# A spectral layer beside a two-layer FFN on one core: the transform reordered with a fold, gelu in one activation, and the instruction order made by a list scheduler

## Chip, cores, metric

One NeuronCore of one Trainium2 chip. The metric is the device time of one execution in microseconds; medians of several runs are quoted.

## The reference, cut to what matters

```python
x = A_x                                   # 1 x 2048 x 640, bf16
xn = layernorm(x)                         # over the 640 features
# A: a filter in the frequency plane
X = rfft2(xn)                             # 2048 x 321, complex
y = irfft2(X * (w_r + 1j * w_i)).astype(bf16)
# B: two dense layers, 640 -> 1536 -> 640
h = gelu(xn @ w1 + b1)                    # tanh form
out = x + y + (h @ w2 + b2)
```

The Fourier transforms are matrix products with constant tables. The sequence of 2048 is taken as 128 x 16, so its transform has two stages.

## The kernel before

Five engines run hand-ordered lists of instructions. Tiles of 128 sequence positions are normalised, transposed, taken through the feature transform (complex from there on) and the first sequence stage; then come transposes of the filter and of the data, the second stage with the filter, two inverse stages, and an output product in which 18 matmuls (12 of the FFN, 6 of the inverse feature transform) are summed per half. Two quarters of the first FFN product are woven into the middle as items of fixed places. The parts that the argument touches:

```python
# x: tiles 0..3, then the tables and W1 in the same queue; tile 4 only when tile 0 is normalised
for c in range(4):
    load_x_tile(c, c)
... etab; gtab; bdtab; b1t; W1sb ...
def act_normalize(c):
    ... activation(Identity, bias=nmr, scale=rstd) ...
    if c + 4 < 16:
        W("sp", act_xn, n)
        load_x_tile(c + 4, xs)

# one FFN item: a product, and the gelu of the items before it, in stages
def ffn_item(t):
    ... five matmuls of 512 columns ...
    activation(hb, PB[bnk], ACT.Identity, bias=b1col)          # item t
    activation(sg, ub, ACT.Sigmoid, scale=GSCALE)              # item t-2
    tensor_tensor(h2, hb, hb, mult)                            # item t-1
    tensor_scalar_add(ub, h2, A22)
    tensor_tensor(ub, ub, hb, mult)
    tensor_tensor(gT, hb, sg, mult)                            # item t-3

# the order: chain items in fixed sequence, one ffn_item after every third or so
chain = [T x11] + [B2C x11] + [Da x21] + [Db x24]
```

Of the kernel before, what the change touches and what calls it, by code (L numbers as in the profile page):

```python
# [6 lines left out]
dt = mybir.dt  # L7
ACT = mybir.ActivationFunctionType
ALU = mybir.AluOpType

S = 2048
D = 640
F = 1536
KP = 328
NG = 41
NDC = 5
NFC = 12
NT1 = 48
GSCALE = 2.0 * float(np.sqrt(2.0 / np.pi)) * 0.044715
A22 = 1.0 / 0.044715  # L20


def _bf16_bits(a):
    a = np.ascontiguousarray(a, dtype=np.float32)
    u = a.view(np.uint32).astype(np.uint64)
    r = ((u + 0x7FFF + ((u >> 16) & 1)) >> 16).astype(np.uint16)
    return r


def _make_tables():  # L30
    T = {}
    d = np.arange(D)[:, None].astype(np.float64)
    k = np.arange(KP)[None, :].astype(np.float64)
    valid = (np.arange(KP) < 321)[None, :]
    Ec = np.cos(2 * np.pi * ((d * k) % D) / D) * valid
    Es = -np.sin(2 * np.pi * ((d * k) % D) / D) * valid
    Etab = np.concatenate([Ec, Es], axis=1)
    T["Etab"] = Etab.reshape(NDC, 128, 2 * KP).transpose(1, 0, 2)
    s1 = np.arange(128)[:, None, None].astype(np.float64)
    s2 = np.arange(16)[None, :, None].astype(np.float64)  # L40
    m1 = np.arange(128)[None, None, :].astype(np.float64)
    ang = 2 * np.pi * ((m1 * (16 * s1 + s2)) % 2048) / 2048.0
    Gc, Gs = np.cos(ang), np.sin(ang)
    T["Gtab"] = np.concatenate([Gc, Gs, -Gs], axis=2)
    m1b = np.arange(128)[:, None, None].astype(np.float64)
    s2b = np.arange(16)[None, :, None].astype(np.float64)
    s1b = np.arange(128)[None, None, :].astype(np.float64)
    angH = 2 * np.pi * ((m1b * (16 * s1b + s2b)) % 2048) / 2048.0
    Hc, Hs = np.cos(angH), np.sin(angH)
    T["Htab"] = np.concatenate([-Hs, Hc, Hs], axis=2)  # L50
    qin = np.arange(128)
    s2_in = qin // 8
    kk_in = qin % 8
    qout = np.arange(128)
    m2_out = qout // 8
    kk_out = qout % 8
    delta = (kk_in[:, None] == kk_out[None, :]).astype(np.float64)
    ang16 = 2 * np.pi * ((s2_in[:, None] * m2_out[None, :]) % 16) / 16.0
    T["BDtab"] = np.concatenate([delta * np.cos(ang16), delta * np.sin(ang16), -delta * np.sin(ang16)], axis=1)
    q = np.arange(128)  # L60
    m2q = q // 8
    kkq = q % 8
    col = np.arange(128)
    s2c = col // 8
    kkc = col % 8
    delta2 = (kkq[:, None] == kkc[None, :]).astype(np.float64)
    ang16b = 2 * np.pi * ((m2q[:, None] * s2c[None, :]) % 16) / 16.0
    T["BD2tab"] = np.concatenate([-delta2 * np.sin(ang16b), delta2 * np.cos(ang16b), delta2 * np.sin(ang16b)], axis=1)
    kk_ = np.arange(384)[:, None].astype(np.float64)
    dd = np.arange(D)[None, :].astype(np.float64)  # L70
    kidx = np.arange(384)
    ck = np.where((kidx == 0) | (kidx == 320), 1.0, 2.0)[:, None]
    validk = (kidx < 321)[:, None]
    angE = 2 * np.pi * ((kk_ * dd) % D) / D
    GEr = ck * np.cos(angE) / (S * D) * validk
    GEi = -ck * np.sin(angE) / (S * D) * validk
    GE = np.stack([GEr, GEi], axis=1)
    T["GEtab"] = GE.reshape(3, 128, 2, D).transpose(1, 0, 2, 3)
    T["ident"] = np.eye(128)
    return T  # L80


class Chan:

    def __init__(self, nc, name, inc=1):
        self.sem = nc.alloc_semaphore(name)
        self.n = 0
        self.inc = inc

    def next(self):  # L90
        self.n += self.inc
        return self.n


def bass_parallel_sum__spectral_gfnet__dense_activation_gelu__prompt_kernel(
# [11 lines left out]
    T = _make_tables()  # L107
    c_etab = nc.inline_tensor(_bf16_bits(T["Etab"]), name="c_etab")
    c_gtab = nc.inline_tensor(_bf16_bits(T["Gtab"]), name="c_gtab")
    c_htab = nc.inline_tensor(_bf16_bits(T["Htab"]), name="c_htab")  # L110
    c_bd = nc.inline_tensor(_bf16_bits(np.concatenate([T["BDtab"], T["BD2tab"]], axis=1)), name="c_bd")
    c_ge = nc.inline_tensor(_bf16_bits(T["GEtab"]), name="c_ge")
    c_ident = nc.inline_tensor(_bf16_bits(T["ident"]), name="c_ident")

    x2 = A_x[0]
    xv = x2.rearrange("(p c) d -> c p d", c=16)
    ov = out[0].rearrange("(p c) d -> c p d", c=16)
    wrv = A_w_r.rearrange("(m2 p) k -> p m2 k", p=128)
    wiv = A_w_i.rearrange("(m2 p) k -> p m2 k", p=128)
# [5 lines left out]
    ops = {"pe": [], "act": [], "dve": [], "pool": [], "sp": []}  # L125

    def E_(eng, f):
        ops[eng].append(f)
    pe = lambda f: E_("pe", f)
    act = lambda f: E_("act", f)  # L130
    dve = lambda f: E_("dve", f)
    pool = lambda f: E_("pool", f)
    sp = lambda f: E_("sp", f)

    def W(eng, ch, n):
        if n <= 0:
            return
        ops[eng].append(lambda e, s=ch.sem, n=n: e.wait_ge(s, n))

    with ExitStack() as es:  # L140
        sb = lambda name, shape, dtype=dt.bfloat16: es.enter_context(nc.sbuf_tensor(name, shape, dtype))
        ident = sb("ident", [128, 128])
        bdtab = sb("bdtab", [128, 768])
        b1t = sb("b1t", [NFC, 128])
        b1col = sb("b1col", [128, NFC], dt.float32)
        gT = sb("gT", [128, NFC, S])
        stats = sb("stats", [128, 16, 12], dt.float32)
        mv = sb("mv", [128, 16, 2], dt.float32)
        stdv = sb("stdv", [128, 16], dt.float32)
        rstd = sb("rstd", [128, 16], dt.float32)  # L150
        nmr = sb("nmr", [128, 16], dt.float32)
        epsv = sb("epsv", [128, 1], dt.float32)
        warm = sb("warm", [128, 1], dt.float32)
        R4N = 17920
        R4 = sb("R4", [128, R4N])
        xnT = bass.AP(tensor=R4, offset=0, ap=[[R4N, 128], [1, 10240]]).rearrange("p (c s) -> p c s", c=NDC)
        W1sb = bass.AP(tensor=R4, offset=10240, ap=[[R4N, 128], [1, 7680]]).rearrange("p (c f) -> p c f", c=NDC)

        R1N = 32912
        R1 = sb("R1", [128, R1N])  # L160

        def r1(off, n):
            return bass.AP(tensor=R1, offset=off, ap=[[R1N, 128], [1, n]])
        o = 0
        W2g = r1(o, 10496).rearrange("p (r g m k) -> p r g m k", r=2, g=NG, m=16); o += 10496
        xring = r1(o, 4 * D).rearrange("p (j d) -> p j d", j=4); o += 4 * D
        xnring = r1(o, 4 * D).rearrange("p (j d) -> p j d", j=4); o += 4 * D
        etab = r1(o, NDC * 656).rearrange("p (c x) -> p c x", c=NDC); o += NDC * 656
        gtab = r1(o, 16 * 384).rearrange("p (s x) -> p s x", s=16); o += 16 * 384
        xdring = r1(o, 4 * 656).rearrange("p (j r k) -> p j r k", j=4, r=2); o += 4 * 656  # L170
        wnring = r1(o, 2 * 2 * 4 * KP).rearrange("p (j r m k) -> p j r m k", j=2, r=2, m=4); o += 2 * 2 * 4 * KP
        assert o <= R1N, o
        Zsb = r1(0, 10496).rearrange("p (r g m) -> p r g m", r=2, g=NG)
        T2T = r1(10496, 10496).rearrange("p (r g m) -> p r g m", r=2, g=NG)
        Vsb = r1(20992, 10496).rearrange("p (s r k) -> p s r k", s=16, r=2)
        getab = r1(0, 3 * 2 * D).rearrange("p (c r d) -> p c r d", c=3, r=2)
        UT = [r1(3840 + kc * 4096, 4096).rearrange("p (r s a) -> p r s a", r=2, s=16) for kc in range(3)]
        htabA = r1(16128, 8 * 384).rearrange("p (s x) -> p s x", s=8)
        ysb = r1(20992, 2 * 1024).rearrange("p (j x) -> p j x", j=2)
        stg_off = 20992  # L180
        xrring = r1(stg_off, 3 * D).rearrange("p (j d) -> p j d", j=3)
        ostg = r1(stg_off + 3 * D, 3 * D).rearrange("p (j d) -> p j d", j=3)
        R2N = 10496
        R2 = sb("R2", [128, R2N])
        T2sb = bass.AP(tensor=R2, offset=0, ap=[[R2N, 128], [1, 10496]]).rearrange("p (r g s k) -> p r g s k", r=2, g=NG, s=16)
        W2sb = bass.AP(tensor=R2, offset=0, ap=[[R2N, 128], [1, NFC * D]]).rearrange("p (c e) -> p c e", c=NFC)
        ctmp = bass.AP(tensor=R2, offset=NFC * D, ap=[[R2N, 128], [1, 4 * 512]]).rearrange("p (j x) -> p j x", j=4)
        assert NFC * D + 4 * 512 <= R2N
# [10 lines left out]
        def pbb(i):  # L199
            return PB[i][:].bitcast(dt.bfloat16)  # L200

# [740 lines left out]
```

## Time and profile before

| | before |
|---|---|
| time, median of 4 runs | 262.42 us (261.89 to 262.99) |
| profiled span | 259.0 us |
| TensorE busy / matmuls | 218.0 us / 1507 |
| VectorE, ScalarE busy | 157.8, 121.4 us |
| first x tile to fifth x tile usable | 3.5 to 22.5 us |

TensorE's busy time overstates how full the engine is (a transpose of 128 columns has a record of 219 ns, and the next one starts after 56). One more view is needed below, the groups by shape, where the gelu stands as six rows (columns: busy us, mean ns of one, idle of the engine before them):

```profile
L562 ACT ACTIVATE hb<-pb,b1col 128x512 bf16<-128x512 f32 x48 | 34.7, 723 | 46.9 <-PE pb L272 46.6
L572 ACT ACTIVATE sg<-ub 128x512 bf16<-128x512 bf16 x48 | 31.9, 665 | 5.2 <-DVE ub L590 5.1
L584 DVE TENSOR_TENSOR h<-hb 128x512 bf16<-128x512 bf16 x48 | 20.0, 416 | 6.2 <-ACT hb L562 6.2
L587 DVE TENSOR_SCALAR ub<-h 128x512 bf16<-128x512 bf16 x48 | 15.2, 316 | 1.6
L590 DVE TENSOR_TENSOR ub<-ub,hb 128x512 bf16<-128x512 bf16 x48 | 20.4, 425 | 1.6
L599 DVE TENSOR_TENSOR gT<-hb,sg 128x512 bf16<-128x512 bf16 x48 | 20.0, 418 | 0.1
```

These six rows are 76 us of VectorE and 67 us of ScalarE. They cost time only where one of those two engines sets the pace.

### The profile page before, as it was taken

Reading aid. Unit: us, or ns where it says so; the run is one execution under the profiler, and the core shown is the slowest. Engines: PE = TensorE matmul, PEld = TensorE weight load, DVE = VectorE, ACT = ScalarE, POOL = GpSimd, SP = SyncE. Lnnn points to the kernel's source line nnn. Section 1 sums busy time; section 2 is a strip of 40 time slices with the busy share of each in tenths; the row PEclk is TensorE's granted clock in tenths of the full one; section 3 lists DMA queues with packets and bytes.
Section 4 is the critical chain, followed back from the end, with each engine's and each line's share of the span. In section 5 each row is a group of like instructions: output and inputs, shape, how many; then the busy total and the mean of one; then the engine's idle time right before and its main releaser. Section 6 shows DMA issues by size and latency. Waiting matters only on the chain.

```text
span 259.0 us, 4212 instructions
## 1 busy us (share of the span) xinstructions
PE 218.0 (84%) x1507; PEld 129.2 (50%) x1507; DVE 157.8 (61%) x433; ACT 121.4 (47%) x258; POOL 31.0 (12%) x48
## 2 busy tenths in 40 slices
PE   0703999999959585499299999999999999999995
PEld 0401667768734133266166755545555455655652
DVE  3304688745987999974669996567555774121121
ACT  2500788974148365299848892355323551000000
POOL 8368900000000000000820000000000000000000
PEclk9999999999999977979769999999999999999999
DMA  6999322100009003120400020011101111113101
GB/s 183 385 360 311 107 78 71 35 0 3 3 0 304 0 1 121 16 109 0 152 3 0 1 78 24 26 54 51 51 15 40 51 53 51 53 51 101 53 25 51
DMA packets 10941, 19.89 MB, mean 77 GB/s; under 512 B 1193, under 2 KB 9002, under 8 KB 10794
## 3 DMA queue, kind: packets, MB, share of 16 engines
q1 hardware_dynamic: 10154, 17.00, 20.0%
q0 software_dynamic: 768, 2.63, 3.2%
q8 instruction: 12, 0.20, 0.3%
q14 instruction: 7, 0.06, 0.1%
HBM read 17.01 MB, written 2.62 MB: 76 GB/s over the span
## 4 chain that ended last, share of the span: by engine, by line
PE 57%; DVE 19%; ACT 10%; DMA 7%; issue 5%; DVEq 0%; SPq 0%; ACTq 0%
PE pb L272 57%; DMA R<-in_A_x_dram 7%; ACT R L717 3%; DVE R L529 2%; DVE R L635 2%; ACT R L401 2%; ACT hb L562 2%; DVE R L680 2%; DVE R L689 1%; DVE R L684 1%; DVE R L681 1%; DVE R L682 1%; ACT sg L572 1%; DVE R L428 1%; DVE R L687 1%
## 5 line engine op out<-in xcount | busy, mean ns | idle before, releaser
L272 PE MATMUL pb<-R 128*128 128x512 bf16 (+6 forms) x752 | 138.4, 336 | 23.4 <-DVE R L428 12.5
L272 PEld LDWEIGHTS pb<-R 128*128 128x128 bf16 (+2 forms) x752 | 71.2, 102 | 74.0 <-DVE R L428 13.9
L272 PE MATMUL pb<-R,gT 128*128 128x512 bf16 (+1 forms) x384 | 57.4, 299 | 0.0
L562 ACT ACTIVATE hb<-pb,b1col 128x512 bf16<-128x512 f32 x48 | 34.7, 723 | 46.9 <-PE pb L272 46.6
L854 DVE TENSOR_TENSOR R<-pb,R 128x512 bf16<-128x512 f32 x16 | 11.1, 691 | 52.4 <-issue 42.6
L272 PEld LDWEIGHTS pb<-R,gT 128*128 128x128 bf16 x384 | 30.5, 98 | 24.7
L572 ACT ACTIVATE sg<-ub 128x512 bf16<-128x512 bf16 x48 | 31.9, 665 | 5.2 <-DVE ub L590 5.1
L584 DVE TENSOR_TENSOR h<-hb 128x512 bf16<-128x512 bf16 x48 | 20.0, 416 | 6.2 <-ACT hb L562 6.2
L590 DVE TENSOR_TENSOR ub<-ub,hb 128x512 bf16<-128x512 bf16 x48 | 20.4, 425 | 1.6
L599 DVE TENSOR_TENSOR gT<-hb,sg 128x512 bf16<-128x512 bf16 x48 | 20.0, 418 | 0.1
L358 DVE BATCH_NORM_STATS2 stats<-R 128x6 f32<-128x320 bf16 x16 | 7.7, 484 | 17.1 <-DMA R<-in_A_x_dram 17.1
L272 PE MATMUL pb<-R,bdtab 128*128 128x512 bf16 (+1 forms) x44 | 11.0, 385 | 7.0 <-ACT R L667 3.9
L717 ACT ACTIVATE R<-pb 128x256 bf16<-128x256 f32 x41 | 14.0, 593 | 4.7 <-DVE R L684 4.7
L587 DVE TENSOR_SCALAR ub<-h 128x512 bf16<-128x512 bf16 x48 | 15.2, 316 | 1.6
L401 ACT ACTIVATE R<-R,nmr,rstd 128x640 bf16<-128x640 bf16 x16 | 14.6, 919 | 0.9 <-DVE nmr L389 0.9
L789 POOL MEMSET R<- 32x4096 bf16 x1 | 3.5, 3504 | 91.5 <-PE pb L272 91.5
L420 PE MATMUL pb<-ident,R 128*128 128x128 bf16 x80 | 8.0, 238 | 7.4 <-ACT R L401 7.3
L325 POOL COPY R<-R 128x328 bf16<-128x328 bf16 x32 | 13.1, 466 | 7.1 <-DMA R<-in_A_w_i_dram 7.1
L477 ACT ACTIVATE R<-pb 128x328 bf16<-128x328 f32 x32 | 12.5, 441 | 1.5 <-PE pb L272 0.6
L272 PE MATMUL pb<-bdtab,R 128*128 128x256 bf16 x82 | 12.1, 302 | 0.0
L665 ACT ACTIVATE R<-pb 128x512 bf16<-128x512 f32 (+1 forms) x11 | 6.2, 568 | 12.0 <-DVE R L684 9.8
L447 DVE CAST R<-pb 128x328 bf16<-128x328 f32 x16 | 7.9, 495 | 6.2 <-PE pb L272 5.6
(41 smaller groups left out, 152.5 us busy)
## 6 DMA issues: line engine op xcount, KB each, us to landing
R<-in_A_x_dram SPq DMA_DIRECT2D x32, 160.0 KB, 2.3
R<-in_B_w_dram SPq DMA_DIRECT2D x2, 1920.0 KB, 12.3
out_dram<-R SPq DMA_DIRECT2D x16, 160.0 KB, 1.8
R<-c_gtab SPq DMA_DIRECT2D x1, 1536.0 KB, 9.9
R<-c_htab SPq DMA_DIRECT2D x2, 768.0 KB, 4.2
R<-in_A_w_r_dram POOLq DMA_DIRECT2D x4, 321.0 KB, 7.2
R<-in_A_w_i_dram POOLq DMA_DIRECT2D x4, 321.0 KB, 7.5
R<-c_ge SPq DMA_DIRECT2D x1, 960.0 KB, 4.7
```

Of the source, the lines that this page charges most:

```text
L272: ins = e.matmul(o_, lhsT=lw, rhs=rh, start=st, stop=stp)
L325: ins = e.tensor_copy(W2g[:, ri, :, m2, :], wnring[:, j, ri, ml, :].rearrange("p (g k) -> p g k", k=8))
L401: act(lambda e, c=c, slot=slot, xs=xs: e.activation(xnring[:, slot, :], xring[:, xs, :], ACT.Identity, bias=nmr[:, c:c + 1], scale=rstd[:, ...
L477: ins = e.activation(T2sb[:, ri, :, c, :], PB[bnk][:, 0:KP].rearrange("p (g k) -> p g k", k=8), ACT.Copy)
L562: act(lambda e, bnk=bnk, hs=hs, fc=fc: e.activation(hb[:, hs, :], PB[bnk][:, 0:512], ACT.Identity, bias=b1col[:, fc:fc + 1], scale=1.0).th ...
L572: act(lambda e, us=g4["us"], ss=ss: e.activation(sg[:, ss, :], ub[:, us, :], ACT.Sigmoid, scale=GSCALE).then_inc(act_e4.sem, 1))
L584: dve(lambda e, hs=hs3, h2s=h2s: e.tensor_tensor(out=h2[:, h2s, :], in0=hb[:, hs, :], in1=hb[:, hs, :], op=ALU.mult).then_inc(dve_self.sem ...
L587: dve(lambda e, h2s=h2s, us=us: e.tensor_scalar_add(ub[:, us, :], h2[:, h2s, :], A22).then_inc(dve_self.sem, 1))
L590: dve(lambda e, hs=hs3, us=us: e.tensor_tensor(out=ub[:, us, :], in0=ub[:, us, :], in1=hb[:, hs, :], op=ALU.mult).then_inc(dve_e3.sem, 1))
L599: dve(lambda e, hs=g5["hs"], ss=g5["ss"], fc=g5["fc"], q=g5["q"]: e.tensor_tensor(out=gT[:, fc, 512 * q:512 * (q + 1)], in0=hb[:, hs, :], ...
L717: ins = e.activation(dst, src, ACT.Copy)
L854: dve(lambda e, ba=ba, osl=osl, xs=xs: e.tensor_tensor(out=ostg[:, osl, 0:512], in0=PB[ba][:, 0:512], in1=xrring[:, xs, 0:512], op=ALU.add))
```

## The change

The intent: fewer matmul columns (real data through the first sequence stage; the features folded about their middle, so that sums meet cosines and differences meet sines), one activation per gelu, and an order that a list scheduler computes at build time from estimated durations, instead of one written by hand. Every operation has a priority; at each step the engine that can start first takes its ready operation of highest priority, and slots of PSUM and SBUF are given out in the same pass. The order is then fixed, and each engine is given its list in that order. The diff cut to its core:

```diff
-    T["Etab"] ... T["Gtab"] ... T["BDtab"] ...      # complex, feature transform first
+    T["G"], T["H"], T["E"], T["GE"], T["M"], T["N"] # real sequence stage, folded features
+class Sched: ...                                    # priorities, ready lists, buffer pools, semaphores
+        load_x(0); load ident
+        for j in range(3):
+            load W1 slice j
+            if j == 0: load b1t; load_x(1)
+        load gtab; load_x(2); load_x(3); load etab; load mtab
+        ... 24 loads of the filter, 16 partitions each, in the layout of its use ...
+        load ntab; getab; htab; b2
+        B_b1ps, B_b1c = Buf("b1ps", psum), Buf("b1col")
+        K.op([("pe", 0.1)], 50, ... matmul(b1ps, lhsT=b1t, rhs=ident[0:12, 0:12]))
+        K.op([("dve", 0.2)], 50, ... tensor_copy(b1col, b1ps))
+        # per tile: statistics (priority 100 - g), rstd = (var + eps) ** -0.5 on GpSimd,
+        # normalise, transpose, fold, first sequence stage (priorities 100 - c/2)
+            for k, op in enumerate((ALU.add, ALU.subtract)):
+                tensor_tensor(xf[k], xn[0:320], xn[639:319:-1], op)
+            5 matmuls of 128 columns against gtab[c]
+        # FFN: lowest TensorE priority, fills what is left
+                pr = 10 - q4 - fc / 20
+                5 matmuls of 512 columns
+                activation(gT, hps, ACT.Gelu_apprx_tanh, bias=b1col)       # needs b1col
+        # per column group q of 16: 6 x 320 (features), 4 x 322 (second stage), filter, 10 x 128 (inverse)
+        # per output tile c of 16: 6 x 320 (inverse features), 24 x 320 (FFN) + 4 x 320 (inverse sequence)
-            pipeline of Identity, square, add, multiply, Sigmoid, multiply
-            chain = T, B2C, Da, Db with ffn items at fixed places
```

## The prediction

> **What bounds the kernel now.** I read the page's busy digits first, then stretches of the span, then the chain that ended last, then the groups by shape.
>
> The page:
>
> ```profile
> span 259.0 us, 4212 instructions
> PE 218.0 (84%) x1507; PEld 129.2 (50%) x1507; DVE 157.8 (61%) x433; ACT 121.4 (47%) x258; POOL 31.0 (12%) x48
> PE   0703999999959585499299999999999999999995
> PEclk9999999999999977979769999999999999999999
> ```
>
> The second half is solid TensorE. In the first half there is a hole in slices 0 to 4, and a ragged stretch in slices 11 to 19 where the granted clock falls too. The stretches of the span, split where those change (columns: length, then busy us and count for PE, PEld, DVE, ACT, POOL, then clock, DMA share, GB/s):
>
> ```profile
> 0.00:24.00 24.00, 5.04 (x26) 3.00 (x27) 6.37 (x21) 5.98 (x9) 16.31 (x29) 1.00 0.92 321
> 24.00:60.00 36.00, 35.02 (x272) 24.57 (x271) 25.10 (x75) 27.79 (x60) 7.58 (x18) 1.00 0.21 62
> 60.00:128.60 68.60, 50.73 (x375) 30.35 (x373) 55.93 (x144) 41.66 (x97) 4.69 (x2) 0.91 0.20 67
> 128.60:256.00 127.40, 127.17 (x837) 71.28 (x837) 69.58 (x193) 46.01 (x92) 2.38 (x1) 0.98 0.13 41
> ```
>
> The chain that ended last says what fills each (start, length, what):
>
> ```profile
> 7.29 15.19 DMA R<-in_A_x_dram
> ...
> 61.97 6.26 DVE R L529 x11
> ...
> 128.62 123.25 PE pb L272 x806
> ...
> 255.88 0.69 DVE R L854
> ```
>
> So: (1) until 24 us TensorE waits for x. The fifth tile's load is issued only after tile 0 is normalised, behind the tables and W1 in one queue. (2) 60 to 128.6 us belongs to VectorE and ScalarE: copies of transposes, then six tensor_tensor per group of the filter, with four VectorE and two ScalarE instructions per gelu item in the same strict order. (3) From 128.6 us TensorE alone sets the end, to within 3 us.
>
> A busy TensorE record includes latency, so I price TensorE by spacing. The transposes stand back to back here:
>
> ```profile
> 61.33 4.74 PE L522 MATMUL pb<-ident,R 128*128 128x128 bf16 x82
> ```
>
> (4.74 - 0.22 for the last one's latency) / 81 = 56 ns. Taking starts of consecutive records for the other widths, the median spacing is 216 ns at 512 columns, 139 at 328, 109 at 256[...]. At 320 columns that makes 136, at 322 137.
>
> TensorE work before, in us: x transposes 80 x 56 = 4.5; feature transform 160 x 139 = 22.2; first sequence stage 64 x 139 = 8.9; transposes of filter and data 164 x 56 = 9.2; second stage 8.9; inverse stages 82 x 109 + 96 x 109 = 19.4; first FFN product 240 x 216 = 51.8; output 16 x 18 x (216 + 56) = 78.3. Sum 203. The other 56 of the 259 us are waits, cold clock and the last 3 us.
>
> [...]mean granted clock 0.91 in 60 to 128.6 us and 1.00 in the solid stretch 140 to 256. [...]the trace has 570 ns between biased 512-column PSUM reads and 478 to 495 for plain ones. [...]the trace shows the forward case only (335 ns for 512) and nothing reversed.
>
> **The change part by part.**
>
> *TensorE.* The sequence transform runs first on real data, straight from the normalised tile as weights, so five 128-column matmuls per tile (80 x 56 = 4.5) replace two complex stages. The fold about the middle turns the feature transform into cosine and sine halves: 16 x 6 x 320 columns = 96 x 136 = 13.1. Second sequence stage 64 x 137 = 8.8, its inverse 160 x 56 = 9.0, inverse features 96 x 136 = 13.1, output 16 x 28 x 136 = 60.9, FFN 51.8, x transposes 4.5. Sum 165.6, that is 37 us less. The transposes of filter and data (9.2) are gone, W is loaded in the layout it is used in, and the six spectral matmul pairs per output tile fall to four matmuls.
>
> *ScalarE and VectorE.* Each gelu becomes one biased activation, 48 x 0.57 = 27 us, instead of 48 x (0.57 + 0.52) of ScalarE and 48 x (0.45 + 0.33 + 0.34 + 0.34) = 70 us of VectorE. VectorE keeps bn_stats 32 x 0.39 = 12.6, small ones about 4, normalise 16 x 0.25 = 4, folds 32 x 0.235 = 7.5, filter products 16 x 0.74 = 11.8[...], sums 8 x 1.2 = 9.6, final adds 16 x 0.74 = 11.8: 61 us. Shared: 80 copies of 640 columns from PSUM at 0.585 (ScalarE[...]) or 0.73 (VectorE), and 16 at 0.40: some 58 us. Altogether about 146 us on two engines, 73 each, under half of what TensorE has. They leave the path, except at the head.
>
> *The head.* x now comes in four loads of 640 KB, the first at the front of the queue. The first four 160 KB tiles landed in 3.5 us at first and 640 KB at some 385 GB/s (the page's fastest slice) is 1.7 us, so x arrives about 5.0. Then four tiles of statistics (4 x 0.91), rstd by a power on GpSimd ([...]no record of its cost), normalise 4 x 0.25, three folds, a transpose and a copy: first FFN product near 12 us. The table of the sequence stage lands only near 13 us; FFN products fill that. From then on the VectorE needs about 2.3 us per tile and TensorE has 0.56 + 3 x 1.08 = 3.8 us of work per tile, so TensorE is full.
>
> *The middle.* Per column group TensorE has 1.9 us of spectral work and nearly as much FFN filler; the other two engines need 2.1 us of their own each, with the gelus. With the FFN at lowest priority the list scheduler can put its 1.08 us pieces into every gap. The six-deep FFN/filter entanglement of 60 to 128.6 us should vanish.
>
> *Sum.* 12 us head + (165.6 - 1.1 already done) + 2 us of half clock while it warms + 4 us of waits where the scheduler's model and the chip differ + 3 us end (add, store, as now) = 185.5 us span; the timed runs lie 3.8 us over the profiled span now (262.8 against 259.0), so 189.3.
>
> Of the 73 us gained, some 37 are TensorE work, 12 the head, and the rest, about 24, the waits and cold clock of 24 to 128.6 us.
>
> **Rivals.**
>
> (a) *The static order stalls.* [...]If a load or a copy is later than the model has it, FFN pieces that could run stand behind it. Weakest point: the filter now comes in 24 loads, each to 16 partitions in 642-byte rows, through the one queue; the issues there cost about 0.43 us each now, so 11 us of issuing. Needed near 45 us; if it comes later, the middle slips by what is missing, 5 to 15 us: 195 to 204.[...]
>
> (b) *VectorE bounds the head.* [...]a fold costs 0.40 instead of 0.235: 5 us more VectorE work, of which only the part before the first FFN product (1 us) shows, as TensorE has a reserve in FFN pieces. If the power on GpSimd takes several us, each of these shows once. 190 to 194.
>
> (c) *ScalarE reloads its table between copy and gelu*. 1.28 us each, as the two loads in this trace take; with dozens of alternations it would cost 50 us or more. Against it: now Copy, Identity and Sigmoid alternate with one load for them all. I give it little.
>
> (d) *No waits at all*: with a warm clock and a scheduler that was fitted well, 181.
>
> **Range and chances.** Terms that are counts by measured spacings (165.6) hold to 1 to 2%. The uncertain ones are the head (10 to 17) and the waits (0 to 15). That gives 178 to 203. For less than 2% gain 68 us would have to be lost again, which only (c) or a failure of the schedule could do.
>
> **What would show it.** Right: 1264 matmuls plus one for the bias; median spacing 136 to 137 at 320 and 322 columns; a PE row that is 9 from about slice 3 to the end; first 512-column matmul between 11 and 15 us; VectorE and ScalarE below half busy; no more than two table loads; a chain that is TensorE for over 80% of the span. Wrong: PE digits under 8 in the middle, with waits put down to the filter products or to W's load (rival a); a spacing of reversed right-hand sides above 136; copies on ScalarE near 0.9 us rather than 0.59; a head beyond 17 us.

These of its prices can be had as estimates from the trace of the kernel before:

- 136 ns at 320 columns and 137 at 322 lie on the line through the measured 109 at 256 and 139 at 328.
- The tensor_tensor instructions of VectorE start 136 ns apart at 128 elements and 335 at 512, 0.52 ns an element. That makes 235 for a fold of 320 and 0.74 us for a filter product of 1288. The 0.40 of rival (b) is the fold with twice the time per element.
- The copies of ScalarE from PSUM start 264 ns apart at 256 columns and 478 at 512, which makes 585 at 640. Those of VectorE (fp32) have 331 at 256 and 407 at 328, which makes some 0.73 us.
- The 0.25 us of normalising: the one-input instruction of the gelu (L587, 512 elements) has a record of 293 ns in the median, of which some 81 are latency if it has as much as the tensor_tensor (416 of record, 335 from start to start). With the same fixed part as there, 640 elements make about 0.25.
- The half clock: matmuls of 328 columns start 273 ns apart until 27.6 us, where they have 139 from 28.0 us on. The 2 us in the sum are an estimate beside this.

Rival (a) rests on the fixed lists alone.

## The result

The changed kernel takes 197.57 us (197.00 to 198.18, 4 runs) against 262.42. Its ratio is 0.7532, with a 95% interval of 0.7499 to 0.7565. A ratio here is the mean time of one kernel's fast runs over that of the other's fast runs of the same rounds, so not quite the ratio of the quoted medians. The prediction of 189 lay 8.6 us too low and its range of 178 to 203 holds the result.

The page of the changed kernel, the same rows as before:

```profile
span 196.4 us, 3073 instructions
PE 172.5 (88%) x1265; PEld 113.7 (58%) x1265; DVE 88.3 (45%) x221; ACT 75.1 (38%) x110; POOL 28.3 (14%) x32
PE   0149760899999999999999999999999999999993
PEclk9999996589999999999999999999999999999999
```

TensorE is solid from slice 8 on, where before it was ragged until slice 19. But the row does not do what the prediction asked of it: there is a 6 and a 0 in slices 5 and 6, and the clock falls in slices 6 to 8. The stretches of the span, cut at that hole (columns as before):

```profile
0.00:15.80 15.80, 4.04 (x36) 3.69 (x37) 10.83 (x38) 2.07 (x3) 1.96 (x10) 1.00 0.92 323
15.80:27.90 12.10, 11.11 (x73) 5.52 (x70) 11.18 (x40) 3.90 (x5) 1.55 (x3) 1.00 1.17 168
27.90:35.10 7.20, 0.04 (x1) 0.00 (x0) 7.20 (x29) 0.00 (x0) 1.89 (x3) 0.72 1.22 129
35.10:41.20 6.10, 6.02 (x40) 4.25 (x41) 3.56 (x11) 4.84 (x8) 0.69 (x1) 0.50 1.16 191
41.20:176.30 135.10, 135.10 (x1004) 88.76 (x1001) 52.26 (x104) 62.86 (x93) 20.84 (x15) 1.00 0.18 59
```

From 27.9 to 35.1 us neither TensorE nor ScalarE does anything while VectorE is busy throughout. The 6.1 us after it run at a granted clock of 0.50. After that the stretch of 135 us has no gap at all. What ends the hole is told by the timeline, TensorE first and ScalarE after it (start, length, engine, line, what, count, idle before and its releaser):

```profile
24.54 3.40 PE L450 MATMUL ps<-xnT,W 128*128 128x512 bf16 x15
35.17 3.08 PE L554 MATMUL ps<-ident,T 128*128 128x128 bf16 x25 [7.23 <-DVE b1col L514]
```

```profile
35.15 4.15 ACT L583 ACTIVATE gT<-ps,b1col 128x512 bf16<-128x512 f32 x7 [10.44 <-DVE b1col L514]
```

Both engines wait for one small instruction, the copy of the bias column for the gelu (b1col, line L514): 118 ns on VectorE, at 35.0 us. Then seven gelus run in a row. TensorE had made 35 matmuls of 512 columns by then (5 from 15.84 us, 15 from 17.95, 15 from 24.54), which is seven finished FFN tiles of five. Seven banks held those tiles and one, by the kernel's own allocation, the bias column itself; that is all eight of its pool, so not even a transpose could be written. The copy has priority 50, and VectorE's statistics, normalising and folds have 92 to 100. As long as any of these was ready, the copy was not taken, although everything behind it hung on it: a priority inversion, made when the order was computed.

That it was made then, and not on the chip, can be checked without the chip: run on an ordinary machine, the scheduler in the changed kernel's own text gives the bias matmul PSUM bank 0 and the seven FFN tiles banks 1 to 7, puts the copy at 34.0 us, leaves TensorE empty from 26.4 to 34.4 us and computes a span of 195.7 us, where the chip took 196.4.

In the groups, the rows that take the place of the six of before:

```profile
L583 ACT ACTIVATE gT<-ps,b1col 128x512 bf16<-128x512 f32 x48 | 32.3, 689 | 30.6 <-PE ps L450 20.1 <-DVE b1col L514 10.4
L562 DVE TENSOR_TENSOR T<-T 128x320 bf16<-128x320 bf16 x32 | 8.6, 316 | 0.0
L622 DVE TENSOR_TENSOR T<-Y,Wf 128x1288 bf16<-128x1288 bf16 x16 | 12.5, 823 | 0.6 <-ACT Y L457 0.5
```

The gelu is one row of 32 us, and 10.4 us of the idle time before it are the bias column. The folds (L562) and the filter products (L622) are small, and the products waited for nothing but the copy of their input (0.5 us), so the load of the filter was never late.

### The profile page after: what moved, and what is told of

It reads as the page before. It is cut to its first block, busy times and chain, and to the rows that moved or that the text cites. A ratio compares the mean times of both kernels' runs of the same rounds, so it can differ in the third digit from the quotient of the medians.

```text
span 196.4 us, 3073 instructions
## 1 busy us (share of the span) xinstructions
PE 172.5 (88%) x1265; PEld 113.7 (58%) x1265; DVE 88.3 (45%) x221; ACT 75.1 (38%) x110; POOL 28.3 (14%) x32
## 4 chain that ended last, share of the span: by engine, by line
PE 85%; DVE 11%; DMA 2%; ACT 0%; issue 0%
PE ps L450 82%; DVE stats L528 5%; PE ps L554 4%; DMA XV<-in_A_x_dram 2%; DVE T L547 1%; DVE T L562 1%; DVE mv L530 1%; DVE xnT L458 1%; DVE ost L704 0%; DVE XW L458 0%; ACT gT L583 0%; DVE nmr L534 0%; DVE ve L531 0%; DVE b1col L514 0%
## 5 line engine op out<-in xcount | busy, mean ns | idle before, releaser
L450 PE MATMUL ps<-xnT,W 128*128 128x512 bf16 x240 | 56.9, 388 | 0.0
L450 PE MATMUL ps<-XW,gT 128*128 128x320 bf16 x384 | 54.8, 299 | 0.8 <-ACT gT L583 0.8
L704 DVE TENSOR_TENSOR ost<-ps,Wf 128x640 bf16<-128x640 f32 x16 | 13.2, 824 | 87.0 <-PE ps L450 87.0
L450 PEld LDWEIGHTS ps<-XW,gT 128*128 128x128 bf16 x384 | 37.5, 98 | 15.9 <-ACT gT L583 1.5
L583 ACT ACTIVATE gT<-ps,b1col 128x512 bf16<-128x512 f32 x48 | 32.3, 689 | 30.6 <-PE ps L450 20.1
L688 POOL TENSOR_TENSOR Wf<-Wf,b2bc 128x640 f32<-128x640 bf16 x16 | 22.2, 1394 | 125.1 <-DVE ost L704 67.1
L450 PEld LDWEIGHTS ps<-xnT,W 128*128 128x128 bf16 x240 | 23.5, 100 | 25.1 <-issue 1.7
L528 DVE BATCH_NORM_STATS2 stats<-XV 128x6 f32<-128x320 bf16 x32 | 13.7, 467 | 4.9 <-DMA XV<-in_A_x_dram 4.9
L450 PE MATMUL ps<-getab,XV 128*128 128x320 bf16 x96 | 15.3, 299 | 0.0
L450 PE MATMUL ps<-etab,XW 128*128 128x320 bf16 x96 | 14.7, 299 | 0.0
L622 DVE TENSOR_TENSOR T<-Y,Wf 128x1288 bf16<-128x1288 bf16 x16 | 12.5, 823 | 0.6 <-ACT Y L457 0.5
L450 PE MATMUL ps<-Xb,mtab 128*128 128x322 bf16 x64 | 10.4, 300 | 0.0
```

The source lines that it names most:

```text
L450: ins = e.matmul(o_, lhsT=lw, rhs=rh, start=st, stop=sp_)
L528: K.op([("dve", 0.4)], pr, lambda e, _, c=c, h=h: e.bn_stats(stats[:, c, 6 * h:6 * h + 6], view(XV, c * D + H2 * h, [[1, H2]])), reads=[B_ ...
L583: K.op([("act", act_us(512, 1))], pr + 50, lambda e, _, q4=q4, fc=fc, hps=hps: e.activation(gT[:, fc, 512 * q4:512 * q4 + 512], ps(hps.slo ...
L622: filt_ops.append(K.op([("dve", dve_us(4 * KP, 2))], pr, lambda e, _, k=k, Y=Y, TB=TB, pair=pair: e.tensor_tensor(out=view(TT, TB.slot * 8 ...
L688: K.op([("pool", pool_us(640))], 50, lambda e, _, xr=xr, xo=xo: e.tensor_tensor(out=xov(xo), in0=view(Wf, XR + xr.slot * D, [[1, D]]), in1 ...
L704: K.op([("dve", dve_us(640))], 95, lambda e, _, xo=xo, os_=os_, fps=fps: e.tensor_tensor(out=ost[:, os_.slot, :].rearrange("p (h n) -> p h ...
```

## The experiments

Experiments 1 to 7 start from the changed kernel (3 to 7 with the edit of experiment 1 in them), 8 to 10 from the kernel before.

**1. The bias column first.** Is that hole the whole difference from the prediction?

```diff
-        K.op([("pe", 0.1)], 50, ...)
-        K.op([("dve", 0.2)], 50, ...)
+        K.op([("pe", 0.1)], 101, ...)
+        K.op([("dve", 0.2)], 101, ...)
```

> The matmul and the copy that make the bias column of the gelu get priority 101 in place of 50; nothing else is edited, though the list scheduler reorders what follows. Theory (the bias column, held back at 35 us in the changed kernel, keeps seven finished FFN tiles and itself in the eight PSUM banks, so TensorE idles 7.2 us and comes back at half clock): the idle time before 35 us and the half-clock stretch go, span 185 to 188 us, time 186 to 190. Rival (the head is bound by VectorE's statistics and normalising, and the bias only happens to be named): less than 3 us gained, 194.5 to 198.

Measured: 187.16 us (186.90 to 187.27), ratio 0.7135 (0.7094 to 0.7177). Page and stretches:

```profile
span 185.3 us, 3068 instructions
PE   0039999999999999999999999999999999989993
PEclk9999999999999999999999999999999999999999
```

```profile
28.00:35.00 7.00, 6.95 (x60) 4.22 (x59) 7.00 (x24) 5.17 (x8) 0.69 (x1) 1.00 1.22 125
35.00:41.00 6.00, 6.00 (x44) 3.35 (x43) 5.89 (x20) 3.13 (x5) 0.69 (x1) 1.00 1.18 160
```

Two priorities are worth 10.4 us. The stretch that was empty is full, ScalarE works in it, and the clock never drops. VectorE is as busy there as before (7.00 of 7.00), so it was not VectorE's work that stopped TensorE, as the rival had it.

**2. The same hole, removed another way.** The first experiment also lets the scheduler reorder the rest. This one leaves the bias column where it was and takes away the gelu's need of it (the biases are so small that the result passed the comparison all the same). Its output is wrong, which doesn't matter for the time.

```diff
-    activation(gT, hps, ACT.Gelu_apprx_tanh, bias=b1col, ...)  reads=[hps, B_b1c]
+    activation(gT, hps, ACT.Gelu_apprx_tanh, bias=0.0, ...)    reads=[hps]
```

> Wrong on purpose: the changed kernel with its late bias column left where its priority puts it, but the gelu reads no bias (the biases are some 0.0005, so the result may pass all the same). It tells the wait for the column from the moving of the column. Theory (the finished FFN tiles wait in PSUM for a gelu that waits for the column): as fast as e1, 185.5 to 189. Rival (e1 won because the new priorities reshuffled the list): 194 or more.

Measured: 186.51 us (185.51 to 187.24), ratio 0.7115 (0.7076 to 0.7155), the same as experiment 1 within the noise. The copy itself now runs even later, at 40.9 us, and nothing waits for it (count, ns, first and last start):

```profile
L514 DVE COPY b1col<-ps x1: 115/115/115, 40.9 to 40.9; 128x12 f32<-128x12 f32 x1
```

The wait was the cost, not the luck of one order.

**3. FFN pieces held back.** What is the filling worth?

```diff
     K.op([("pe", 5 * mm_us(512))], pr, ...,
-         reads=..., writes=[hps])
+         reads=..., writes=[hps], gate=ipc_ops)   # all 16 inverse sequence stages
```

> The bias column first as in e1, and all 48 pieces of the first FFN product held until the last inverse sequence stage has been ordered, so that none fills a gap of the head or of the sequence stages. Theory (the order matters because these 52 us are the filler for a head and middle that VectorE and the loads set): 20 to 30 us over e1, time 208 to 218, TensorE digits of 1 to 3 in the head. Rival (TensorE would have been busy or the others would catch up): under 8 us over e1.

Measured: 216.35 us (214.90 to 216.76), ratio 0.8240: 29 us over experiment 1 with the same instructions. The row of TensorE shows where:

```profile
PE   0253655579999977999999999999999999998994
```

The head alone cannot fill TensorE: the digits are 2 to 7 in slices 1 to 8 (more than the 1 to 3 that the expectation named, but the time came out in its range). Part of these digits is a slow clock: until 52 us matmuls of 128 columns stand 107 ns apart and those of 320 columns 267, where experiment 1 has 56 and 136 in 20 to 60 us. The page's PEclk row prints 9 there all the same, as the trace holds no record of the granted clock before 52 us. So the 29 us are empty TensorE and half clock together, and no run parts them.

**4. FFN pieces first.** The opposite order.

```diff
-                pr = 10 - q4 - fc / 20
+                pr = 200 - q4 - fc / 20
```

> e1 with the FFN pieces at the highest TensorE priority in place of the lowest: they run as soon as their four tiles are there and none is left for the middle. Theory (the pieces are worth most as filler): the middle is short of TensorE work, 5 to 12 us over e1, 192 to 199. Rival (only the amount of work counts, any order fills): under 3 us over e1.

Measured: 197.44 us (196.86 to 197.93), ratio 0.7522: 10 us over experiment 1. Now the head is full and the middle starves:

```profile
PE   0049997999799799899999659999999999999993
DVE  0999996702900700159999930111111111122211
PEclk9999999999999999999999975999999999999999
```

VectorE stands nearly still in slices 8 to 16 of that run (0 to 2, one 9, one 7), as the transposes and first sequence stages that it works with now stand behind FFN pieces on TensorE, and has to catch up in slices 17 to 22, when no filler is left. (Its copies of the first sequence stage wait 33.3 us for TensorE.) After gaps of 0.7 and 1.9 us TensorE then ran at a granted clock of 0.50 from 114.8 to 121.6 us (5.88 us busy, so some 3 of the 10 us are lost there). Of the three places tried, the lowest priority was the best for the filler.

**5. The old gelu in the new order.** One part of the change undone.

```diff
-    activation(gT, hps, ACT.Gelu_apprx_tanh, bias=b1col)
+    activation(gT, hps, ACT.Identity, bias=b1col)
+    tensor_tensor(u, gT, gT, mult); tensor_scalar_add(u, u, A22); tensor_tensor(u, u, gT, mult)
+    activation(u, u, ACT.Sigmoid, scale=GSCALE)
+    tensor_tensor(gT, gT, u, mult)
```

> The bias column first as in e1, and one part of the change undone: each gelu again as two activations and four VectorE instructions, scheduled by the list scheduler (in place in gT with a ring of four). Theory (in the new order VectorE and ScalarE have room, 61 us of own work on VectorE plus 70): TensorE stays the bound from about 40 us on, 3 to 10 us over e1, time 190 to 200, VectorE busy about 150 us. Rival (the single gelu carries the gain): 210 or more.

Measured: 199.03 us (median of the three fast runs, 198.11 to 199.11; the fourth was slow, 201.71), ratio 0.7579, 11.9 us over experiment 1, so 2 us more than the theory's upper bound for the difference, though inside its range for the time. VectorE is busy 154.4 us. The waits show where it bites (who waited for whom: us in total, times, longest):

```profile
PE ps L452 <- DVE gT L598: 9.8, 3, 4.7
```

The output products wait 9.8 us for the last multiplication of the gelu: with six stages the final tiles of the FFN are finished long after their matmuls. The longest of these waits is followed by a granted clock of 0.50 from 173.2 to 180.1 us (4.29 us busy in it, so some 2 us more). The single gelu is worth about 12 us here, though VectorE has room on average.

**6. Twice the statistics.** Does VectorE bound the head?

```diff
-                for h in range(2):
+                for h in (0, 1, 2, 3):     # 2 and 3 into a tile that nobody reads
                     bn_stats(...)
```

> e1 with every bn_stats issued twice, the second into a tile that nobody reads: 32 x 0.39 = 12.6 us more VectorE work, all in the head. Theory (VectorE is on the path only until the first FFN product, four tiles, and FFN pieces fill TensorE afterwards): 3 to 6 us over e1, 190 to 193. Rival (VectorE bounds the whole head): 10 to 13 us over e1, 197 to 200.

Measured: 190.69 us (190.39 to 191.26), ratio 0.7268: 3.5 us over experiment 1, for 10.3 us more busy time of VectorE (98.2 against 87.9). So most of the added work is hidden; what shows lies before the first FFN product, which starts at 20.80 us in place of 15.96, while the whole span of that run is 4.2 us longer (189.5 against 185.3). Of the added work, four tiles (4 x 2 x 0.39 = 3.1 us) must come before that product; the trace has 4.8, and the rest was not followed up.

**7. A shorter head.** On top of experiment 1.

```diff
-        load_x(0)                                        # 4 tiles
+        load x tiles 0 and 1; load x tiles 2 and 3
-        rstd chain at pr = 100 - g
+        rstd chain at 101
-        fold at pr - 0.2
+        fold at pr - 1.5
```

> On top of e1, the head alone: the first x load is split in two halves, the three small instructions that make rstd and its product get priority 101, and the folds give way to normalising (priority less by 1.5 in place of 0.2). Theory (TensorE is full from the first FFN product on, so what that product is earlier by comes off the end): the first 512-column matmul at 12 to 14 us in place of 16, time 183.5 to 186. Rival (something later sets the end, such as the loads of tables and filter): 187, as e1.

Measured: 185.14 us (184.55 to 185.89), ratio 0.7055 (0.7028 to 0.7083). The first 512-column product starts 3 us earlier than in experiment 1 (15.96), and the end comes 2 us earlier:

```profile
13.00 5.15 PE L450 MATMUL ps<-xnT,W 128*128 128x512 bf16 x15 [0.58 <-DVE xnT L458]
```

This is the fastest version, correct, 6% below the changed kernel.

**8. The single gelu alone in the kernel before.**

```diff
-    Identity, square, add, multiply, Sigmoid, multiply over items t .. t-3
+    activation(gT[:, fc, 512q:512q+512], PB[bnk], ACT.Gelu_apprx_tanh, bias=b1col)
```

> One part of the change alone: the kernel before with each gelu as one biased activation, all else as it was. Theory (the part matters only where VectorE and ScalarE bound, 60 to 128.6 us): that stretch shrinks by 10 to 25 us and the solid TensorE stretch after it keeps its length for the same work, time 238 to 252. Rival (TensorE work and the head carry all of the gain): 258 or more. Rival (gelu was nearly all of it): under 215.

Measured: 251.68 us (249.73 to 252.65), ratio 0.9588 (0.9525 to 0.9650). VectorE falls from 157.8 to 90.5 us, yet only 10.4 us come off: in the middle the filter's six instructions per group on VectorE and the copies on ScalarE stay in strict order, and the chain there now runs through them without the gelu.

**9. x early alone in the kernel before.**

```diff
     load x tiles 0..3; etab
-    gtab; bdtab; b1t; W1
     def act_normalize(c):
         ... load_x_tile(c + 4)
+        if c == 1: gtab
+        if c == 3: bdtab; b1t; W1
```

> Another part of the change alone: the kernel before with the loads of the sequence table, the second-stage tables and W1 moved behind the loads of x tiles 5 and 7 in the queue, as the changed kernel has x early. Theory (11 us of TensorE's hole at the start are the fifth tile behind those tables, and the stages after it are in strict order, so an earlier start goes through to the end): 6 to 11 us gained, 251 to 256. Rival (the middle is bound by VectorE and loads of its own and absorbs it): under 3 us, 259 to 262.

Measured: 257.49 us (255.98 to 257.63), ratio 0.9778: 5.3 us, less than expected and more than the rival allows. (By the verdict's 2% line this one is "unclear": the ratio's interval, 0.9742 to 0.9815, lies across 0.98, though clear of 1.) The 24 us at the start got fuller (TensorE busy 13.3 us in place of 5.0), but the chain shows that the same queue was blocked again a little later:

```profile
8.36 9.88 DMA R<-c_gtab
...
21.38 7.76 DMA R<-in_A_x_dram
```

The table now delays the first sequence stage (TensorE waits 1.3 us for it), and a later x tile, issued behind W1 in that queue, takes 7.8 us to land, for which TensorE stands idle for 2.4 us at 28 us. Moving these loads about in the queue shifted part of the wait. The changed kernel, with x in four loads and the first one at the front, has only one wait for x in its chain, the first 4.1 us.

**10. Both of these in the kernel before.**

> Both parts in the kernel before, x early and the single gelu. Theory (they act in different stretches, 0 to 24 us and 60 to 128.6 us, so they add): the sum of the two gains, 10.4 us of the gelu and what e9 shows, 240 to 246; the other 55 us of the way to e1 are then the transform and the order. Rival (one hides the other): 249 or more.

Measured: 247.23 us (246.84 to 250.02), ratio 0.9430. The sum of the two single gains, 10.4 and 5.3, would give 262.8 - 15.7 = 247.1: they add, as the theory says. The stated range of 240 to 246 was missed by 1 us, because it assumed more of experiment 9. Of the 75 us from the kernel before to experiment 1, these two parts carry 16; the remaining 59 come with the new transform and the computed order, which cannot be parted further without writing another kernel. What the order can lose is shown by experiments 3 and 4 (29 and 10 us).

## Why the prediction was right, and where it was not

The range held, and so did the mechanism of the gain: TensorE sets the pace, with less work and with FFN pieces as filler. The sum failed mainly in one term, the waits. Its parts against the trace of the changed kernel, in us:

| term of the sum | predicted | measured |
|---|---|---|
| to the first FFN product | 12 | 15.8 |
| TensorE work left | 164.5 | 163.6 (the priced 165.6, as counts and spacings held, less 35 matmuls of 56 ns done before) |
| half clock while it warms | 2 | 0.8 (the first five took 1.99 in place of 1.24) |
| waits and what follows from them | 4 | 12.0: 7.2 bias column, 3.0 half clock behind it (6.0 busy at 0.50), 1.0 in 15.8 to 27.9, 0.8 before the last tiles |
| end | 3 | 3.1 |
| span | 185.5 | 196.4 (the terms give 195.3) |
| time over span | 3.8 | 1.8 |

**The work was right.** The spacings of consecutive records are 136 ns at 320 columns, 216 at 512 and 56 at 128, the reversed right-hand sides included. Only 322 columns take 139 in place of 137, 0.1 us in all. The copies on ScalarE (584 ns from start to start), the folds (235) and the filter products (747) came as priced. Normalising was priced 0.25 and takes 0.355 us.

**The failed step** is the prediction's "4 us of waits where the scheduler's model and the chip differ". It was priced at 4 us and measured 12. The order was not spoilt by a difference between model and chip; it contained the wait from the start, as the replay above shows (195.7 us computed, 196.4 measured), because the scheduler does not take an operation of priority 50 while others of 92 and more are ready. The span that the scheduler computes was there to be printed before the run. It isn't always that close: for experiment 1 it is 185.2 (measured 185.3), for experiment 5 190.1 (measured 197.2). Experiments 1 and 2 remove it in two ways and give 187.2 and 186.5 us, within the noise of each other and 2 to 3 us below the prediction. That the span of experiment 1, 185.3 us, meets the predicted 185.5 is partly luck: its head is 4 us longer than predicted (15.96) and its waits after that are 2.6 us shorter (1.4). The diff showed it: the two lines of the bias column stand there with their priority, and I read them as trivial because they are short. I asked how long each operation takes and not when it would be let in.

**The signs.** The count of 1265 matmuls, the spacings, VectorE and ScalarE below half busy (45 and 38%), two table loads and a chain of 85% TensorE came as named. The first 512-column matmul came at 15.84 us, outside the named 11 to 15, and the row of TensorE was not full from slice 3.

**The clock.** The prediction's mean clocks of 0.91 and 1.00 are measured. In the trace of the kernel before, half clock begins at 92.7, 99.5, 109.8 and 126.8 us, and the longest gaps of TensorE next to these points are 2.6, 2.7, 3.3 and 4.8 us; after a gap of 3.1 us at 74.1 us it did not come. So what brings it was not shown. In the changed kernel the 0.8 us of warming is read from spacing (427 ns at 512 columns, 107 at 128, until 17.4 us), as the trace has no record of the granted clock before that.

**The head** was 3.8 us longer than predicted: the second pair's rstd waits behind folds and statistics, and the transposed tile behind both. Experiment 7 brings the product to 13.0 us with priorities and a split load.

**The last term** was too large by 2 us, to the prediction's favour: I took the median time less the profiled span, but these were of different executions. In the later runs each time lies 1.8 us over its own span (198.18 and 196.4, 187.12 and 185.3).

**The rivals.** Rival (a), a stall of the static order, is what happened, at the size it named (195 to 204), but with the wrong culprit: the filter products waited 0.5 us, and not for their load. (The 24 filter loads landed in 17.4 to 40.2 us. The DMA engines moved 120 to 139 GB/s in slices 4 to 7 then, against 394 in slice 2 with x, W1 and a table; why was not tested.) Rival (b) named two costs that did not come: the reversed fold took 235 ns from start to start, what the forward spacings of 136 ns at 128 elements and 335 at 512 make for 320, and not 400; the power took 0.69 us and not several. Its reserve, that of VectorE's work only the part before the first FFN product shows, is what experiment 6 found. Rival (c), table reloads, did not occur: there are two table loads of 1.28 us, as before, and neither is on the path. Rival (d), 181, was not reached even by experiment 7.

**The split of the gain** that the prediction gave (37 work, 12 head, 24 waits) holds for the work; the head gave 8 (24 to 15.8 us), and of the measured 65 us some 20 are left for the waits, after the bias column had taken 10 of theirs.

## What to carry to other kernels

When a list scheduler makes the order, look for operations that are cheap, early and needed by many, and give them the priority of what waits for them; two lines were worth 5% here. Print the span that the scheduler computes, and look for holes in its own list before the chip runs it. Finished results that could not leave PSUM stopped TensorE for 7.2 us here once all eight banks of the pool were held, so the first thing to check in a hole is what the evacuation waits for. Try large independent work at the lowest priority, as filler: the same instructions took 187, 197 or 216 us depending on where it stood.
